# Transposing a batch step's five softmax tiles in one TensorE session of two 64-row tiles, with wide PSUM evictions

## The chip, the core and the metric

The kernel runs on one core of one Trainium2 chip. The metric is the time of one execution on the device in microseconds (us); the kernel before takes 783.63 us, the median of three runs (782.31 to 784.8).

## What is computed

Two independent problems, A and B, are computed and their outputs joined along the last axis. Each is a grouped-query attention block on bf16 data: batch 16, 80 query rows, model width 576, 32 query heads on 16 key/value heads, 512 cached keys, head width 128.

```
q = (x @ wq).reshape(B, Sq, Hq, Dh).transpose(0, 2, 1, 3)
k, v = jnp.repeat(k_cache, 2, axis=1), jnp.repeat(v_cache, 2, axis=1)
p = softmax(einsum("bhqd,bhkd->bhqk", q, k) * Dh ** -0.5, axis=-1)
o = einsum("bhqk,bhkd->bhqd", p, v)
out = o.transpose(0, 2, 1, 3).reshape(B, Sq, Hq * Dh) @ wo
```

## The kernel before

The work is cut into 128 batch steps (U in the code; 64 a problem). A batch step takes one batch entry and four key/value heads. Each key/value head serves two query heads of 80 rows, so it has 160 query rows; the first 128 of them make one score tile of 128 x 512 (k = 1 to 4 in the code, one a head), and the four remainders of 32 rows are put together into a fifth tile (k = 0). So there are 5 x 128 = 640 score tiles.

A tile goes through these stages:

- **QK** on TensorE into a score bank of PSUM: line 658 for k = 1 to 4, and lines 644 to 647 for k = 0, where four matmuls work in four 32-column tiles of the array side by side. Two batch steps' k = 0 tiles are done in one such session.
- **Maximum** on VectorE (line 667), **exponential** with the row sum on ScalarE (line 671, from PSUM to a P tile in SBUF), **reciprocal** of the row sums on VectorE (line 677), **normalisation** of P on GpSimd (line 680).
- **Transposition** of P: four 128x128 TensorE transposes into one PSUM bank (line 686), and one 512-column copy on VectorE from there to pT (line 692 for k = 0, line 694 for k = 1 to 4). For 62 of the 128 batch steps the k = 0 tile is transposed by a DMA from SBUF to SBUF that SyncE issues (line 698).
- **PV** on TensorE (line 731): four matmuls of 160 columns a head, accumulated over the keys; ScalarE copies the result of two heads to oT (line 747).

Around that, TensorE makes the Q projection (line 540: five matmuls of 160 or 480 columns a piece, evicted on ScalarE or VectorE, lines 551 and 552) and the output projection (line 781: 16 matmuls of 288 columns a piece, evicted by lines 793 and 809). K is transposed by DMA on its way in (line 612) and V is loaded plainly (line 616), both issued by SyncE, as are the other loads and the stores.

The order of the instructions on each engine isn't written by hand. Every operation is handed to a planner (`S.add`) with an engine (or two to choose from), a due time in units of one score tile, an estimated duration and, for PSUM, a class of banks. The planner simulates the engines by these estimates, picks the operation that is due first among those that are ready, assigns the banks, and then works out the semaphore waits. An engine runs its list strictly in that order. `BANKS` (line 38) says which of the eight PSUM banks a class may have: S for score tiles, T for transposed tiles, O for PV, M for the projections. `LA` is how many tiles ahead QK runs; `NPA`, `NPR` and `NPT` are the numbers of buffers of P (k = 1 to 4), P (k = 0) and pT.

Of the kernel before, what the change touches and what calls it, by code (L numbers as in the profile page):

```python
# [6 lines left out]
BF16 = mybir.dt.bfloat16  # L7
# [9 lines left out]
NPA = 8  # L17
NPR = 4
NPT = 3
# [28 lines left out]
RDC = 0.78  # L48
RDK = 3.0
RDO = 6.0  # L50
RDD = 1.2
PTO = 0.0
OEO = 0.0
OVO = 0.0
# [19 lines left out]
def _mm(n, cols):  # L74
    return n * (cols * MM1 + MM0)
# [248 lines left out]
def bass_concat_heads__gqa_block_cached__gqa_block_cached__near_ridge_kernel(  # L324
# [9 lines left out]
    B, SQ, D = A_x.shape  # L334
# [12 lines left out]
    NROW = 8 * SQ  # L347
# [4 lines left out]
    with ExitStack() as es:  # L352
        block = es.enter_context(nc.Block())
        sb = lambda name, shape, dt: es.enter_context(nc.sbuf_tensor(name, shape, dt))
        ident = sb("ident", [128, 128], BF16)
# [14 lines left out]
        ps = es.enter_context(nc.psum_tensor("ps", [128, 8, 512], F32))  # L370
        psb = ps[:].bitcast(BF16)
# [3 lines left out]
        sem_names = (["e_pe", "e_act", "e_dve", "e_pool", "d_x00", "d_x01", "d_x10", "d_x11", "d_wo",  # L375
                      "d_wq0", "d_wq1", "d_wqs", "d_wqt"]
                     + ["d_out%d" % i for i in range(NOSB)]
                     + ["d_r%d" % i for i in range(NPT)]
                     + ["d_k%d" % i for i in range(NK)] + ["d_v%d" % i for i in range(NV)])
# [32 lines left out]
        def em_warmend(e):  # L412
# [4 lines left out]
              name="warm", stream="W", dur=NWARM * 0.427, alloc=[vw])  # L417
# [3 lines left out]
        def em_warm2(e, vw=vw2):  # L421
            last = None
            for _ in range(NWARM2):
# [71 lines left out]
        for goct in range(NG):  # L495
            prob, q, half = unit(goct)
# [29 lines left out]
            for i in range(8):  # L526
                for c in range(2):
# [35 lines left out]
                    S.add(("act", "dve"), x + 0.4, em_qev, reads=[R(vb, 0)],  # L563
# [39 lines left out]
        for U in range(NSU):  # L603
# [20 lines left out]
            rdma = RDMA[0] <= U < RDMA[1] and U % 4 in RPER and not any(a_ <= U < b_ for a_, b_ in RSKIP)  # L624
            for k in range(5):
# [7 lines left out]
                tq = Q - LA + 0.0  # L633
                vb = S.bank("S")
                vt = S.bank("T")
# [37 lines left out]

                rg = [g_ for g_ in RG[rdma] if k in g_][0]

# [7 lines left out]
                def em_tr(e, psl=psl, vt=vt):  # L683
                    last = None
                    for j in range(4):
                        last = e.transpose(psb[:, vt.phys, j * 128:(j + 1) * 128],  # L686
                                           p_sb[:, psl, j * 128:(j + 1) * 128], ident[:])
                    return last

                def em_ptev(e, k=k, gl=gl, vt=vt, pts=pts):  # L690
                    if k == 0:
                        return e.tensor_copy(pT[:, pts, :, 4, :],  # L692
                                             psb[:, vt.phys, 0:512].rearrange("p (j n) -> p j n", j=4))
                    return e.tensor_copy(pT[:, pts, :, 0:4, gl * 32:gl * 32 + 32],  # L694
                                         psb[:, vt.phys, 0:512].rearrange("p (j h c) -> p j h c", j=4, h=4))

                def em_rtr(e, psl=psl, pts=pts):
                    return e.dma_start_transpose(pT[:, pts, :, 4, :], p_sb[:, psl, :])

                pt_writes = [R(("pT", pts, g4, "R"), U) for g4 in range(4)] if k == 0 else [R(("pT", pts, gl, "A"), U)]  # L700
# [12 lines left out]
                if k == 0 and rdma:  # L713
                    S.add("sp", max(tg + RDK, 5.0 * (U - NPT) + 7.0), em_rtr, reads=[R(("P", psl), ("n", T))], writes=pt_writes, dsem="d_r%d" % pts,
                          name="rtr%d" % T, stream="RT", dur=RDD, cost=RDC, ahead=RDO)
                else:
                    S.add("pe", t0, em_tr, reads=[R(("P", psl), ("n", T)), IDENT], writes=[R(vt, 0)],
                          name="tr%d" % T, stream="T", dur=_mm(4, 128), lat=0.2, alloc=[vt])
                    S.add("dve", t0 + 0.44, em_ptev, reads=[R(vt, 0)], writes=pt_writes,
                          name="ptev%d" % T, stream="ptev", dur=0.33, lat=0.13, ahead=PTO)  # L720

                if k >= 1:
                    if gl % 2 == 0:
                        vo = S.bank("O")
                    off = (gl % 2) * 160
                    pr = gl // 2

                    def em_pv(e, gl=gl, vo=vo, off=off, vs=vs, pts=pts):
                        last = None
                        for j in range(4):  # L730
                            last = e.matmul(ps[:, vo.phys, off:off + 160],  # L731
                                            lhsT=v_sb[:, vs, gl, j * 128:(j + 1) * 128],
                                            rhs=pT[:, pts, j, :, gl * 32:gl * 32 + 32], start=(j == 0), stop=(j == 3))
                        return last

                    S.marks[4 * U + gl] = S.add(
                          "pe", t0 + 2.5, em_pv,
                          reads=[R(("V", vs), U), R(("pT", pts, gl, "A"), U), R(("pT", pts, gl, "R"), U)],
                          writes=[R(vo, 0)], name="pv%d.%d" % (U, gl), stream="PV",
                          dur=_mm(4, 160), lat=0.2, alloc=[vo] if gl % 2 == 0 else [])  # L740
                    if gl % 2 == 1:
                        hb = 8 * (q % 2) + 4 * pr

                        def em_oev(e, vo=vo, hb=hb, row=half * NROW + bl * SQ):
                            dst = oT[:, hb:hb + 4, row:row + SQ]
                            src = ps[:, vo.phys, 0:320].rearrange("p (h s) -> p h s", h=4)
                            return e.copy(dst, src)  # L747

                        S.add("act", t0 + 3.1, em_oev, reads=[R(vo, 0)],
                              writes=[R(("oT", half, bl, q % 2, pr), (prob, q // 2))], name="oev%d.%d" % (U, pr),  # L750
                              stream="oev", dur=0.33, ahead=OEO)

# [142 lines left out]
```

## Time and profile before

| | |
|---|---|
| three runs | 782.31, 783.63 and 784.8 us |
| the profiled execution's own time | 784.8 us |
| its span, first to last instruction | 784.8 us |
| instructions | 21118 |
| bytes read from HBM, written to it | 87.46 MB, 2.95 MB |
| busy on TensorE, VectorE, ScalarE, GpSimd | 771.8, 674.6, 611.4, 432.4 us |

In the profile PE is TensorE's matmuls (a transpose is one), PEld its weight loads, DVE VectorE, ACT ScalarE, POOL GpSimd and SPq SyncE's queue. A row of the groups reads: line, engine, operation, what it writes and reads, shapes, how many; then busy us and mean ns of one; then how long the engine sat idle just before these instructions, and who ended that. A row of the timeline reads: start in us, how long it lasts, engine, line, what it does, how many in a row. Instructions of one engine overlap in the pipeline, so a row's duration is longer than the distance to the next start.

### The profile page before, as it was taken

How to read it: one execution, taken by the hardware profiler on the slowest of the kernel's cores; microseconds unless marked ns; L12 is line 12 of the kernel's file. 1: busy time of each engine (PE TensorE's matmuls, PEld its weight loads, DVE VectorE, ACT ScalarE, POOL GpSimd, SP SyncE). 2: the span in 40 equal slices, each digit the busy share in tenths (PEclk: the TensorE clock that was granted, in tenths of full speed). 3: DMA queues.
4: the chain of work that ended last, by engine and by line, in shares of the span. 5: the costliest groups of instructions: out<-in, count | busy, mean ns of one | idle time of the engine just before them, and what ended most of it. 6: DMA issues, size and time to landing. Idle time of an engine off the chain costs nothing.

```text
span 784.8 us, 21118 instructions
## 1 busy us (share of the span) xinstructions
PE 771.8 (98%) x8010; PEld 563.8 (72%) x8010; DVE 674.6 (86%) x1559; ACT 611.4 (78%) x1735; POOL 432.4 (55%) x647
## 2 busy tenths in 40 slices
PE   9999999999999999999999999899999999999998
PEld 5576677777777777777777777576777777777787
DVE  4999988888888889899889999797878888988982
ACT  1878988888888889777778778777887887887770
POOL 1455755565655566555565555564555655655660
PEclk9999999999999999999999999999999999999999
DMA  9999999979999999999999999999999998999951
GB/s 250 232 255 243 240 220 252 204 175 205 223 198 225 208 256 273 246 218 221 207 178 219 208 194 229 247 223 218 230 200 210 201 233 203 256 226 188 209 144 32
DMA packets 395812, 168.67 MB, mean 215 GB/s; under 512 B 309824, under 2 KB 392256, under 8 KB 395712
## 3 DMA queue, kind: packets, MB, share of 16 engines
q1 hardware_dynamic: 394496, 166.14, 97.3%
q8 instruction: 65, 1.06, 0.6%
q10 hardware_dynamic: 1216, 1.18, 0.5%
q14 instruction: 35, 0.29, 0.1%
HBM read 87.46 MB, written 2.95 MB: 115 GB/s over the span
## 4 chain that ended last, share of the span: by engine, by line
PE 89%; DVE 7%; DMA 3%; ACT 1%; SPq 0%; issue 0%; POOL 0%; DVEq 0%
PE ps L540 20%; PE ps L781 19%; PE ps L731 17%; PE ps L686 15%; PE ps L658 12%; DVE negmax L667 4%; PE ps L644 4%; DVE pT L694 2%; DMA pT<-p_sb 1%; DMA wo_sb<-in_B_wo_dram 1%; DMA out_dram<-osb 1%; DVE qT L552 1%; ACT p_sb L671 1%; PE ps L409 0%; PE ps L464 0%; PE ps L424 0%
## 5 line engine op out<-in xcount | busy, mean ns | idle before, releaser
L680 POOL TENSOR_SCALAR p_sb<-p_sb,rinv 128x512 bf16<-128x512 bf16 x640 | 430.0, 692 | 331.2 <-DVE rinv L677 330.8
L671 ACT ACTIVATE p_sb<-ps,negmax 128x512 bf16<-128x512 f32 x640 | 441.2, 694 | 76.4 <-DVE negmax L667 66.5
L667 DVE TENSOR_REDUCE negmax<-ps 128x1 f32<-128x512 f32 x640 | 428.3, 679 | 11.6 <-PE ps L658 6.5
L694 DVE COPY pT<-ps 128x512 bf16<-128x512 bf16 x512 | 210.0, 413 | 17.4 <-PE ps L686 15.6
L731 PE MATMUL ps<-pT,v_sb 128*128 128x160 bf16 x2048 | 219.2, 233 | 5.7 <-ACT p_sb L671 4.1
L686 PE MATMUL ps<-ident,p_sb 128*128 128x128 bf16 x2312 | 222.7, 219 | 1.8 <-DVE pT L694 1.2
L540 PE MATMUL ps<-xT,wq_sb 128*128 128x480 bf16 (+1 forms) x1280 | 213.2, 300 | 0.2
L731 PEld LDWEIGHTS ps<-pT,v_sb 128*128 128x128 bf16 x2048 | 158.3, 98 | 58.0 <-ACT p_sb L671 9.7
L686 PEld LDWEIGHTS ps<-ident,p_sb 128*128 128x128 bf16 x2312 | 163.3, 98 | 37.6 <-DVE pT L694 8.5
L658 PE MATMUL ps<-kT,qT 128*128 128x512 bf16 x512 | 189.3, 380 | 0.9 <-ACT p_sb L671 0.9
L781 PE MATMUL ps<-wo_sb,oT 128*128 128x288 bf16 x1280 | 171.6, 286 | 0.5 <-DMA wo_sb<-in_B_wo_dram 0.5
L540 PEld LDWEIGHTS ps<-xT,wq_sb 128*128 128x128 bf16 x1280 | 107.0, 98 | 61.6 <-issue 3.4
L781 PEld LDWEIGHTS ps<-wo_sb,oT 128*128 128x128 bf16 x1280 | 122.5, 98 | 36.5 <-DMA wo_sb<-in_B_wo_dram 1.0
L747 ACT CAST oT<-ps 128x320 bf16<-128x320 f32 x256 | 108.8, 426 | 42.4 <-PE ps L731 41.7
L671 ACT ACTIVATION_READ_ACCUMULATOR p_sb<-ps,negmax 128x1 f32 x640 | 130.7, 204 | 0.0
L551 ACT ACTIVATE qT<-ps 128x160 bf16<-128x160 f32 (+1 forms) x158 | 63.0, 399 | 31.6 <-PE ps L540 30.7
L552 DVE TENSOR_SCALAR qT<-ps 128x480 bf16<-128x480 f32 (+1 forms) x98 | 55.1, 562 | 25.4 <-PE ps L540 24.4
L658 PEld LDWEIGHTS ps<-kT,qT 128*128 128x128 bf16 x512 | 49.3, 98 | 7.5 <-ACT p_sb L671 4.0
L809 DVE TENSOR_TENSOR osb<-ps,acc 128x288 bf16<-128x288 f32 x40 | 18.3, 457 | 29.6 <-PE ps L781 27.8
L677 DVE RECIPROCAL rinv<-rowsum 128x5 f32<-128x5 f32 (+2 forms) x190 | 32.0, 169 | 12.2 <-ACT p_sb L671 12.2
L644 PE MATMUL ps<-kT,qT 128*32 128x512 bf16 x512 | 39.9, 388 | 0.1
L692 DVE COPY pT<-ps 128x512 bf16<-128x512 bf16 x66 | 27.5, 416 | 4.5 <-PE ps L686 4.4
(19 smaller groups left out, 48.7 us busy)
## 6 DMA issues: line engine op xcount, KB each, us to landing
v_sb<-in_A_v_cache_dram SPq DMA_DIRECT2D x64, 512.0 KB, 4.5
v_sb<-in_B_v_cache_dram SPq DMA_DIRECT2D x64, 512.0 KB, 4.6
wo_sb<-in_A_wo_dram SPq DMA_DIRECT2D x8, 576.0 KB, 7.4
wo_sb<-in_B_wo_dram SPq DMA_DIRECT2D x8, 576.0 KB, 7.0
wq_sb<-in_B_wq_dram SPq DMA_DIRECT2D x4, 1024.0 KB, 7.2
out_dram<-osb SPq DMA_DIRECT2D x40, 72.0 KB, 2.4
wq_sb<-in_A_wq_dram SPq DMA_DIRECT2D x2, 1024.0 KB, 7.2
wq_sb<-in_A_wq_dram ACTq DMA_DIRECT2D x2, 512.0 KB, 7.0
```

The costliest lines, as they stand in the source:

```text
L540: last = e.matmul(ps[:, vb.phys, 0:n1 - n0], lhsT=wq_sb[:, wsl, ck, i * 128:(i + 1) * 128], rhs=xT[:, half, ck, n0:n1], start=(ck == 0), s ...
L551: return e.activation(dst, src, AF.Identity, scale=SCALE)
L644: last = e.matmul(ps[32 * g4:32 * g4 + 32, vb_.phys, :], lhsT=qT[:, qsl_, bl_, g4 * 160 + 128:g4 * 160 + 160], rhs=kT[:, ks_, :, g4 * 128: ...
L658: return e.matmul(ps[:, vb.phys, :], lhsT=qT[:, qsl, bl, gl * 160:gl * 160 + 128], rhs=kT[:, ks, :, gl * 128:(gl + 1) * 128], start=True, ...
L667: return e.tensor_reduce(negmax[:, si:si + 1], ps[:, vb.phys, :], axis=AX.X, op=AluOpType.max, negate=True)
L671: return e.activation(p_sb[:, psl, :], ps[:, vb.phys, :], AF.Exp, bias=negmax[:, si:si + 1], scale=1.0, accum_out=rowsum[:, ss, k:k + 1])
L680: return e.tensor_scalar(p_sb[:, psl, :], p_sb[:, psl, :], rinv[:, ss, k:k + 1], 1.0, op0=AluOpType.mult, op1=AluOpType.mult)
L686: last = e.transpose(psb[:, vt.phys, j * 128:(j + 1) * 128], p_sb[:, psl, j * 128:(j + 1) * 128], ident[:])
L694: return e.tensor_copy(pT[:, pts, :, 0:4, gl * 32:gl * 32 + 32], psb[:, vt.phys, 0:512].rearrange("p (j h c) -> p j h c", j=4, h=4))
L731: last = e.matmul(ps[:, vo.phys, off:off + 160], lhsT=v_sb[:, vs, gl, j * 128:(j + 1) * 128], rhs=pT[:, pts, j, :, gl * 32:gl * 32 + 32], ...
L747: return e.copy(dst, src)
L781: last = e.matmul(ps[:, vb.phys, 0:DC], lhsT=oT[:, hi, rb * 128:(rb + 1) * 128], rhs=wo_sb[:, wi, c3 * DC:(c3 + 1) * DC], start=(hi == 0), ...
```

## The change

All five P tiles of a batch step are transposed in one TensorE session; the DMA transposes are gone. Each 128x128 transpose becomes two transposes of 64 rows: the upper 64 partitions of P are transposed in the upper 64 rows of the array, the lower 64 in the lower rows, with `tile_position` (0, 0) and (64, 0). Each has 128 x 64 outputs. They are issued in 20 pairs, one upper and one lower, 40 matmuls a session. The upper halves of the tiles k = 1 to 4 go to one PSUM bank (16 pieces of 64 columns, 1024 bf16 columns), the lower halves to a second, and both halves of the k = 0 tile (512 columns) to a third. The two row tiles must not write one bank at the same time, so the lower halves start with the k = 0 tile and the upper halves end with it; ahead of the 17th pair the session waits on a semaphore that its own fourth pair raises.

Three copies a batch step take the place of five: two of 1024 columns on VectorE, and one of 512 that the planner may give to ScalarE or VectorE. pT is laid out as 16 blocks of 160 columns, so that a PV matmul reads its 160 columns in one run. All PV matmuls of a batch step wait for all three copies. The reciprocals are taken in groups of three and two tiles everywhere.

The constants go along: 12 P buffers for k = 1 to 4 instead of 8, two pT buffers instead of three, three score banks instead of four, and other bank classes and due times.

```diff
-NPA = 8
+NPA = 12
-NPT = 3
+NPT = 2
-BANKS = dict(S=(0, 1, 2, 6), T=(3, 4), O=(5, 7), M=(7, 5), M0=(7, 5, 6, 3, 4), M1=(7, 6), ML=(7, 5, 6, 0, 1))
+BANKS = dict(S=(0, 1, 2), T=(3, 4, 6), Y=(6, 5), O=(5, 7, 4), M=(7, 5, 6, 3, 4), M0=(7, 5, 6, 3, 4), M1=(7, 6), ML=(7, 5, 6, 0, 1))
-RG = (((0, 1, 2, 3, 4),), ((0,), (1, 2, 3, 4)))
-RDMA = (24, 126)
-RPER = (1, 2, 3)
-RSKIP = ((46, 64),)
+RG = ((0, 1, 2), (3, 4))
+TS0 = 4.5
+PV0 = 5.5
+PVS = 0.8
-PTO = 0.0
-OEO = 0.0
-OVO = 0.0
+PTO = -2.0
+PTE = (('dve',), ('dve',), ('act', 'dve'))
+OEO = 3.0
+OVO = 1.0
...
-        pT = sb("pT", [128, NPT, 4, 5, 128], BF16)
+        pT = sb("pT", [128, NPT, 16, 160], BF16)
...
-                def em_tr(e, psl=psl, vt=vt):
-                    last = None
-                    for j in range(4):
-                        last = e.transpose(psb[:, vt.phys, j * 128:(j + 1) * 128],
-                                           p_sb[:, psl, j * 128:(j + 1) * 128], ident[:])
-                    return last
...
-                def em_rtr(e, psl=psl, pts=pts):
-                    return e.dma_start_transpose(pT[:, pts, :, 4, :], p_sb[:, psl, :])
...
+            ts = 5.0 * U + TS0
+            vx, vz, vy = S.bank("T"), S.bank("T"), S.bank("Y")
+
+            def em_tr(e, psls=tuple(psls), vbs=(vx, vz), vy=vy, U=U):
+                last = None
+                for n_ in range(20):
+                    if n_ == 16:
+                        e.wait_ge(sems["e_tr"], U + 1)
+                    for h in range(2):
+                        k_, j = divmod(n_, 4)
+                        k_ = (k_ + 1 - h) % 5
+                        if k_:
+                            c_ = ((k_ - 1) * 4 + j) * 64
+                            dst = psb[:, vbs[h].phys, c_:c_ + 64]
+                        else:
+                            dst = psb[:, vy.phys, 0:512].rearrange("p (g j c) -> p g j c", g=4, j=4)
+                            dst = dst[:, 2 * h:2 * h + 2, j, :]
+                        last = e.matmul(dst, lhsT=p_sb[64 * h:64 * h + 64, psls[k_], j * 128:(j + 1) * 128],
+                                        rhs=ident[64 * h:64 * h + 64, 64 * h:64 * h + 64], start=True, stop=True,
+                                        is_transpose=True, tile_position=(64 * h, 0))
+                    if n_ == 3:
+                        last.then_inc(sems["e_tr"], 1)
+                return last
...
+                def em_ptev(e, en="dve", h=h, vt=vt, pts=pts):
+                    f = e.copy if en == "act" else e.tensor_copy
+                    if h == 2:
+                        return f(pT[:, pts, :, 128:160], psb[:, vt.phys, 0:512].rearrange("p (n c) -> p n c", n=16))
+                    return f(pT[:, pts, :, 64 * h:64 * h + 64], psb[:, vt.phys, :].rearrange("p (n c) -> p n c", n=16))
...
+                                        rhs=pT[:, pts, 4 * gl + j, :], start=(j == 0), stop=(j == 3))
```

More of the change, by code (lines that the diff above doesn't have):

```diff
@@ L623, in bass_concat_heads__gqa_block_cached__gqa_block_cached__near_ridge_kernel @@
             vo = None
-            rdma = RDMA[0] <= U < RDMA[1] and U % 4 in RPER and not any(a_ <= U < b_ for a_, b_ in RSKIP)
+            psls = []
             for k in range(5):
@@ L712, in bass_concat_heads__gqa_block_cached__gqa_block_cached__near_ridge_kernel @@
                       writes=[R(("P", psl), ("n", T))], name="nrm%d" % T, stream="pool", dur=0.674, lat=0.1)
[L713 to L751, printed above, removed]
@@ new lines, in bass_concat_heads__gqa_block_cached__gqa_block_cached__near_ridge_kernel, with em_pv, em_oev @@
+            for gl in range(4):
+                if gl % 2 == 0:
+                    vo = S.bank("O")
+                off = (gl % 2) * 160
+                pr = gl // 2
+                tp = 5.0 * U + PV0 + PVS * gl
+                def em_pv(e, gl=gl, vo=vo, off=off, vs=vs, pts=pts):
+                    last = None
+                    for j in range(4):
+                        last = e.matmul(ps[:, vo.phys, off:off + 160],
+                                        lhsT=v_sb[:, vs, gl, j * 128:(j + 1) * 128],
+                                        rhs=pT[:, pts, 4 * gl + j, :], start=(j == 0), stop=(j == 3))
+                    return last
+                S.marks[4 * U + gl] = S.add(
+                      "pe", tp, em_pv,
+                      reads=[R(("V", vs), U)] + [R(("pT", pts, h), U) for h in range(3)],
+                      writes=[R(vo, 0)], name="pv%d.%d" % (U, gl), stream="PV",
+                      dur=_mm(4, 160), lat=0.2, alloc=[vo] if gl % 2 == 0 else [])
+                if gl % 2 == 1:
+                    hb = 8 * (q % 2) + 4 * pr
+                    def em_oev(e, vo=vo, hb=hb, row=half * NROW + bl * SQ):
+                        dst = oT[:, hb:hb + 4, row:row + SQ]
+                        src = ps[:, vo.phys, 0:320].rearrange("p (h s) -> p h s", h=4)
+                        return e.copy(dst, src)
+                    S.add("act", tp + 0.6, em_oev, reads=[R(vo, 0)],
+                          writes=[R(("oT", half, bl, q % 2, pr), (prob, q // 2))], name="oev%d.%d" % (U, pr),
+                          stream="oev", dur=0.33, ahead=OEO)
```

31 lines of the change are left out of this document (15 added, 16 removed).

## The prediction

> **What bounds the kernel now.** I read the page first: engine totals, the slices' clock and the chain that ended last.
>
> ```profile
> span 784.8 us, 21118 instructions
> ...
> PE 771.8 (98%) x8010; PEld 563.8 (72%) x8010; DVE 674.6 (86%) x1559; ACT 611.4 (78%) x1735; POOL 432.4 (55%) x647
> ...
> PEclk9999999999999999999999999999999999999999
> ...
> PE 89%; DVE 7%; DMA 3%; ACT 1%; SPq 0%; issue 0%; POOL 0%; DVEq 0%
> ```
>
> TensorE is the bound: it is busy for 98% of the span at full clock, idle for 784.8 - 771.8 = 13.0 us, and it owns 89% of the last chain. What the change is worth is therefore what it does to TensorE's queue, plus whatever stalls it adds to the 13 us. A busy TensorE isn't a TensorE at its peak, though, so I then read the timeline, where the start of a group minus the start of the one before is the time that the queue really gives it. TensorE alone first:
>
> ```profile
> 399.81 0.51 PE L540 MATMUL ps<-xT,wq_sb 128*128 128x160 bf16 x5
> 400.16 0.39 PE L686 MATMUL ps<-ident,p_sb 128*128 128x128 bf16 x4
> 400.38 0.44 PE L731 MATMUL ps<-pT,v_sb 128*128 128x160 bf16 x4
> 400.66 0.38 PE L658 MATMUL ps<-kT,qT 128*128 128x512 bf16 x1
> 400.87 0.44 PE L731 MATMUL ps<-pT,v_sb 128*128 128x160 bf16 x4
> ```
>
> Then all engines, at a place with a four-tile session (L644):
>
> ```profile
> 404.57 0.39 PE L686 MATMUL ps<-ident,p_sb 128*128 128x128 bf16 x4
> ...
> 404.80 0.38 PE L658 MATMUL ps<-kT,qT 128*128 128x512 bf16 x1
> ...
> 405.00 0.42 DVE L694 COPY pT<-ps 128x512 bf16<-128x512 bf16 x1 [0.29 <-PE ps L686]
> 405.01 0.44 PE L731 MATMUL ps<-pT,v_sb 128*128 128x160 bf16 x4
> ...
> 405.34 0.68 DVE L667 TENSOR_REDUCE negmax<-ps 128x1 f32<-128x512 f32 x1
> ...
> 405.94 0.41 DVE L694 COPY pT<-ps 128x512 bf16<-128x512 bf16 x1
> 406.00 0.51 PE L540 MATMUL ps<-xT,wq_sb 128*128 128x160 bf16 x5
> 406.06 0.69 ACT L671 ACTIVATE p_sb<-ps,negmax 128x512 bf16<-128x512 f32 x1
> ...
> 406.44 0.62 PE L644 MATMUL ps<-kT,qT 128*32 128x512 bf16 x8
> ...
> 406.73 0.41 ACT L747 CAST oT<-ps 128x320 bf16<-128x320 f32 x1
> 406.87 0.32 DVE L552 TENSOR_SCALAR qT<-ps 128x160 bf16<-128x160 f32 x1
> ...
> 406.99 0.40 PE L686 MATMUL ps<-ident,p_sb 128*128 128x128 bf16 x4
> 407.04 0.70 ACT L671 ACTIVATE p_sb<-ps,negmax 128x512 bf16<-128x512 f32 x1
> 407.11 0.69 DVE L667 TENSOR_REDUCE negmax<-ps 128x1 f32<-128x512 f32 x1
> ```
>
> A P tile's four transposes take 0.23 us of the queue (404.57 to 404.80), 0.0575 each for 128 columns. A QK matmul takes 0.21 for 512 columns (404.80 to 405.01), four PV matmuls 0.28 for 4 x 160 (400.38 to 400.66): each form runs at the same rate per column, so time on TensorE goes by streamed columns. Eight 512-column matmuls in the four 32-column tiles of L644 take 0.55 (406.44 to 406.99) and not 8 x 0.21: tiles side by side share a stream's time. Changing into that mode costs too: the five 160-column matmuls ahead take 0.44 (406.00 to 406.44) where five take 0.35 elsewhere (399.81 to 400.16), 0.09 more, and the session takes 0.55 - 2 x 0.21 = 0.13 over its two streams. A change in and out is 0.22 us.
>
> **The change, part by part.** The other rows that carry terms:
>
> ```profile
> L671 ACT ACTIVATE p_sb<-ps,negmax 128x512 bf16<-128x512 f32 x640 | 441.2, 694 | 76.4 <-DVE negmax L667 66.5 <-DMA pT<-p_sb 2.2 <-PE ps L686 1.2
> ...
> L686 PE MATMUL ps<-ident,p_sb 128*128 128x128 bf16 x2312 | 222.7, 219 | 1.8 <-DVE pT L694 1.2 <-POOL p_sb L680 0.5
> ...
> L694 DVE COPY pT<-ps 128x512 bf16<-128x512 bf16 x512 | 210.0, 413 | 17.4 <-PE ps L686 15.6
> ...
> L686 PEld LDWEIGHTS ps<-ident,p_sb 128*128 128x128 bf16 x2312 | 163.3, 98 | 37.6 <-DVE pT L694 8.5 <-POOL p_sb L680 2.0 <-DVE pT L692 1.1
> ...
> L552 DVE TENSOR_SCALAR qT<-ps 128x480 bf16<-128x480 f32 x71 | 46.5, 656 | 23.4 <-PE ps L540 22.5
> ...
> L551 ACT ACTIVATE qT<-ps 128x480 bf16<-128x480 f32 x57 | 32.4, 568 | 2.2 <-PE ps L540 1.8
> L551 ACT ACTIVATE qT<-ps 128x160 bf16<-128x160 f32 x101 | 30.6, 304 | 29.4 <-PE ps L540 28.8
> ...
> L552 DVE TENSOR_SCALAR qT<-ps 128x160 bf16<-128x160 f32 x27 | 8.5, 317 | 2.0 <-PE ps L540 1.9
> L644 PEld LDWEIGHTS ps<-kT,qT 128*32 128x32 bf16 x512 | 7.8, 94 | 10.9 <-issue 2.6 <-ACT p_sb L671 1.4 <-ACT oT L747 1.3
> ```
>
> *TensorE, removed.* 2312 / 4 = 578 tiles go through L686 now (the other 62 of 640 by DMA): 578 x 0.23 = 132.9 us, all on the path.
>
> *TensorE, added.* 128 sessions, one a batch step, all 640 tiles in them. A session is 20 pairs; each matmul streams 64 columns, one in the upper and one in the lower 64 rows of the array. No row shows row tiles or a 64-column matmul. Low end for a pair: both at once, half of a 128-column step, 0.029. High end: no sharing and no shorter step, 2 x 0.0575 = 0.115. I take 0.029, since L644's session shows that tiles share a stream and every form goes by its columns: 20 x 0.029 + 0.22 for the change of mode = 0.80, x 128 = 102.4 us. **Net -30.5 us**. A weight load stands ahead of each matmul, 40 of 128 columns a session instead of 20. Loads keep up today at one per 0.0575, and one of 128 columns shows 98 ns against 94 for 32 columns, so a load hardly grows with columns; that a new one can follow every 0.029 in each half is my choice, and the first thing that could be wrong. The wait that the session has on its own fourth pair is for a matmul issued 12 pairs (0.35 us) earlier, and one lasts 219 ns by its row: hidden; uncovered it holds the four last pairs, up to 0.1 x 128 = 13 us.
>
> At this place the Trainium skill speaks against the change: "TensorE: Matmul & The Clock Gate", section "Back-to-back issue gap", has starts of matmuls never closer than about 25 ns, however few columns they have. If that holds over both halves together, 40 matmuls take an estimated 1.0 us, a session 1.22, and the 128 sessions 156 us, so +23 in place of -30.5. Its section "Packing small matmuls" has tiles start about 4 ns apart, which would leave my 0.80 nearly as it is. L644's eight matmuls in 0.55 us agree with the second for column tiles; no run here shows row tiles.
>
> *PV.* pT becomes contiguous over a head group's 160 columns. L731 already takes 0.07 for 160 columns beside 0.0575 for 128, the same rate, so nothing is gained; the matmuls stay 2048.
>
> *VectorE.* Removed are 578 copies at 0.34 (405.00 to 405.34): 196 us. Added are 256 copies of 1024 columns. The two L552 rows give (656 - 317) / 320 = 1.06 ns a column and 147 ns fixed; the 512-column bf16 copy, 413, is then 0.52 ns a column; 1024 columns last 0.68, and 0.08 less in the queue (0.42 lasts, 0.34 passes): 0.60, 154 us. (At 1.06 ns a column it would be 1.15, 294 us: then VectorE, not TensorE, sets the time near 784; I take the copy's own row.) By the order of the built kernel reciprocals go from 190 to 256 (+6 at 0.1) and Q evictions from 27 small and 71 large to 62 and 68 (+7). 675 - 196 + 154 + 13 = 646 us, 85% of the new span, as now.
>
> *ScalarE.* It gets 126 of the 128 third copies (512 columns): by the L551 rows 0.825 ns a column and 172 fixed, 0.59, in the queue 0.10 less (406.73 to 407.04 against 0.41) = 0.49, so +62; fewer Q evictions, -6. 611 + 56 = 667, 88% instead of 78%: hidden, but the cover is thinner.
>
> *DMA, SyncE, GpSimd.* 62 P transposes leave SyncE's queue and the DMA engines:
>
> ```profile
> L698 SPq DMA_TRANSPOSE pT<-p_sb x62: 1188/1212/3551, 162.9 to 748.5; - x62
> ```
>
> That is 62 x 1.2 = 75 us of SyncE's queue, which held later K and V loads. The chain has 3% DMA in all, and the one wait that the rows put down to these transposes is 2.2 us of ScalarE's (L671), so I count nothing for their going. The 640 normalisations stay; GpSimd at 55% covers their new grouping.
>
> *Waits added.* Five tiles must be normalised before a session, and all of its three copies done before PV. On the built order the instructions between a session and its first PV are, typically, four QK and 2.0 to 2.4 us of projections, some 2.7 us by the durations above; two copies back to back with a maximum ahead need 0.2 + 0.6 + 1.2 = 2.0. Usually covered, at a few places not. Score banks fall from four to three. A score tile holds its bank from QK to the end of the exponential, 404.80 to 406.06 + 0.69 = 406.75, 1.95 us; three banks at one tile per 758 / 640 = 1.18 us allow 3.55 (four allowed 4.9). I add 4 us of stalls to the 13.
>
> **Sum:** 784.8 - 30.5 + 4 = 758.3 us for an execution like the profiled one. That was the slowest of the three, 1.2 over the median 783.63; against the median the forecast is **757**.
>
> **Rivals.** (a) *Pairs take 0.0575, in the session itself*: either the halves don't share (40 x 0.029), or the weight load sets the step. For it: 40 loads where 20 were, and no load faster than one per 0.0575 in the trace. Against: L644. Price: 20 x 0.0575 + 0.22 = 1.37, 175.4 us, +42.5, so 784.8 + 42.5 + 4 - 1.2 = 830; slower than now. It decides at a pair of (132.9 / 128 - 0.22) / 20 = 0.041 us; between there and 0.0575 lie times of 787 to 830. (b) *The score banks run out*: a tile that meets a third copy on ScalarE (0.49) and both large copies on VectorE (1.2) holds its bank for 1.95 + 1.7 = 3.65, over the 3.55 allowed, and QK stands at the head of TensorE's queue with all else behind it. A quarter of a microsecond a step gives 128 x 0.25 = 32: 785 to 790. Against it: both engines keep over a tenth of the span idle. (c) *No narrowing and no sharing*, so the change does not do what it says: 40 x 0.0575 + 0.22 = 2.52, 322.6 us, +190: about 976. All forms' rate by columns speaks against it.
>
> **How the numbers follow.** Forecast 0.57, with its own range 742 (the stalls gone) to 775 (the wait on the fourth pair, 13, uncovered, and some more stalls); (a) 0.25; (b) 0.13; (c) 0.05. To leave out no more than 2 in 10 the range runs from 742 to 832. A measurement of this kernel can tell about 0.3% (2.4 us) from no change. Faster: 0.57 and a quarter of (b), 0.60. Within it: 0.04, from (b). Slower: (a), (c) and the rest of (b), 0.36.
>
> **What would show it.** The timeline of one session: 0.58 to 0.65 us from first to last of 40 starts is right, over 0.82 (a pair over 0.041) kills the gain. The copies of 1024 columns: 0.68 lasting, 0.60 passing. TensorE's idle time: about 17 us; 40 or more, with QK waiting for the exponential, is (b). The transposes' share of the last chain must fall from 15%. Wrong would be a pair cadence far from 0.029, or idle time in the tens.

## The result, and the profile after

The changed kernel takes 745.88 us (median of four runs, 745.61 to 747.22), the kernel before 784.05 (782.31 to 784.8) on the same chip: a ratio of 0.9528, 95% interval 0.9507 to 0.9549. That is 38.2 us less; the forecast was 757, 26.6 less than the 783.63 it started from. On a second chip the two took 745.11 and 779.49, a ratio of 0.9565 (0.9546 to 0.9583). Times on the chips differ by some 5 us for the kernel before, so the runs below are compared by their ratio to it or with the changed kernel's 745 to 746. One correction ahead: the changed kernel's profiled run took 747.22 us with a span of 745.5, and the other runs stand 1.7 us or more over their spans too. The profiled execution of before, listed with 784.8 for both, so probably took some 786.5 us; its own time isn't on record. Spans are compared with spans here.

The page of the changed kernel: totals, the chain by engine and by line, and the groups that the change made.

```profile
span 745.5 us, 26156 instructions
...
PE 737.5 (99%) x10818; PEld 509.0 (68%) x10818; DVE 649.7 (87%) x1337; ACT 650.1 (87%) x1829; POOL 435.7 (58%) x647
...
PE 96%; DVE 2%; DMA 1%; ACT 1%; issue 0%; SPq 0%
PE ps L537 23%; PE ps L795 21%; PE ps L745 19%; PE ps L655 15%; PE ps L710 11%; PE ps L641 5%; DMA wo_sb<-in_B_wo_dram 1%; DVE negmax L664 1%; ACT p_sb L668 1%; PE ps L406 0%; DVE qT L549 0%; PE ps L461 0%; PE ps L421 0%; DVE pT L727 0%; DVE xT L465 0%
...
L727 DVE COPY pT<-ps 128x1024 bf16<-128x1024 bf16 x256 | 171.0, 682 | 8.7 <-PE ps L710 8.2
...
L710 PEld LDWEIGHTS ps<-ident,p_sb 64*128 64x128 bf16 x5120 | 81.8, 95 | 33.1 <-issue 9.5
L710 PE MATMUL ps<-ident,p_sb 64*128 64x64 bf16 x5120 | 96.9, 190 | 0.0
...
L726 ACT COPY pT<-ps 128x512 bf16<-128x512 bf16 x126 | 75.5, 599 | 6.8 <-PE ps L710 6.1
```

The chain by line in the kernel before, for comparison:

```profile
PE ps L540 20%; PE ps L781 19%; PE ps L731 17%; PE ps L686 15%; PE ps L658 12%; DVE negmax L667 4%; PE ps L644 4%; DVE pT L694 2%; DMA pT<-p_sb 1%; DMA wo_sb<-in_B_wo_dram 1%; DMA out_dram<-osb 1%; DVE qT L552 1%; ACT p_sb L671 1%; PE ps L409 0%; PE ps L464 0%; PE ps L424 0%
```

TensorE is still the bound, more purely than before: 96% of the last chain instead of 89%, and idle for 745.5 - 737.5 = 8.0 us instead of 13.0. The transposes fell from 15% of the chain (L686 before) to 11% (L710), and the two projections L537 and L795 now carry 44% of it. VectorE went from 675 to 650 us, ScalarE from 611 to 650.

The timeline of TensorE around one session (start, how long it lasts, line, shapes, how many):

```profile
359.70 0.59 PE L655 MATMUL ps<-kT,qT 128*128 128x512 bf16 x2
360.22 0.76 PE L710 MATMUL ps<-ident,p_sb 64*128 64x64 bf16 x40
360.91 1.19 PE L537 MATMUL ps<-xT,wq_sb 128*128 128x480 bf16 x5
361.94 0.59 PE L655 MATMUL ps<-kT,qT 128*128 128x512 bf16 x2
362.37 0.51 PE L537 MATMUL ps<-xT,wq_sb 128*128 128x160 bf16 x5
```

The session of 40 takes 0.69 us (360.22 to 360.91), and the two QK matmuls ahead of it 0.52 (359.70 to 360.22) where two take 0.43 without a change behind them (361.94 to 362.37). So a session costs 0.69 + 0.09 = 0.78 us. The starts inside it, in ns from the first, upper and lower half in turn:

```
0 3  38 41  67 71  96 100  126 129  155 158  184 187 ...  476 479  505 508  534 537  563 566
```

From the second pair on, a pair follows a pair after 29.2 ns, the halves of a pair 3 to 4 ns apart; in all 128 sessions first and last start are 566 to 568 ns apart. There is no gap ahead of the 17th pair: its wait is hidden.

For the whole span I took every step from one TensorE start to the next against the step of unbroken groups (columns / 2.4 + 2.5 ns: 56 ns at 128 columns, 216 at 512). What is over it where the tiling changes, up to 0.096 us, is the change; the rest is stall.

| us | before | after |
|---|---|---|
| unbroken steps | 747.2 | 694.2 |
| of these the transposes of P | 129.1 | 76.3 |
| changes of tiling | 12.3 | 35.2 |
| stalls | 21.2 | 12.0 |
| ahead of the first start, behind the last | 4.1 | 4.1 |
| span | 784.8 | 745.5 |

The gain is 53.0 of stream, less 22.9 for changes of tiling, and 9.2 of stalls. The first two make 30.1; the prediction had 30.5. It had 4 us more of stalls, and there were 9.2 fewer.

Not all of the 21.2 us in the kernel before is waiting. The clock granted to TensorE was 0.5 from 498.80 to 502.21 us of its span; the stretch began within the longest stall (shown under e1), and the steps behind the stall took twice their time: four PV matmuls 0.49 us (499.40 to 499.89) where they take 0.28 elsewhere. From the end of the stall to the end of the stretch that is an estimated 1.4 us. The mean granted clock of that execution was 0.998, and 1.0 in the changed kernel.

### The profile page after: what moved, and what is told of

It reads as the page before. It is cut to its first block, busy times and chain, and to the rows that moved or that the text cites. A ratio compares the mean times of both kernels' runs of the same rounds, so it can differ in the third digit from the quotient of the medians.

```text
span 745.5 us, 26156 instructions
## 1 busy us (share of the span) xinstructions
PE 737.5 (99%) x10818; PEld 509.0 (68%) x10818; DVE 649.7 (87%) x1337; ACT 650.1 (87%) x1829; POOL 435.7 (58%) x647
## 4 chain that ended last, share of the span: by engine, by line
PE 96%; DVE 2%; DMA 1%; ACT 1%; issue 0%; SPq 0%
PE ps L537 23%; PE ps L795 21%; PE ps L745 19%; PE ps L655 15%; PE ps L710 11%; PE ps L641 5%; DMA wo_sb<-in_B_wo_dram 1%; DVE negmax L664 1%; ACT p_sb L668 1%; PE ps L406 0%; DVE qT L549 0%; PE ps L461 0%; PE ps L421 0%; DVE pT L727 0%; DVE xT L465 0%
## 5 line engine op out<-in xcount | busy, mean ns | idle before, releaser
L664 DVE TENSOR_REDUCE negmax<-ps 128x1 f32<-128x512 f32 x640 | 418.3, 681 | 39.6 <-PE ps L655 20.1
L537 PE MATMUL ps<-xT,wq_sb 128*128 128x480 bf16 (+1 forms) x1280 | 205.8, 300 | 0.6 <-DVE qT L549 0.2
L795 PE MATMUL ps<-wo_sb,oT 128*128 128x288 bf16 x1280 | 181.1, 286 | 2.7 <-DMA wo_sb<-in_B_wo_dram 2.7
L745 PE MATMUL ps<-pT,v_sb 128*128 128x160 bf16 x2048 | 180.6, 233 | 0.0
L727 DVE COPY pT<-ps 128x1024 bf16<-128x1024 bf16 x256 | 171.0, 682 | 8.7 <-PE ps L710 8.2
L795 PEld LDWEIGHTS ps<-wo_sb,oT 128*128 128x128 bf16 x1280 | 122.3, 98 | 44.1 <-DMA wo_sb<-in_B_wo_dram 2.9
L537 PEld LDWEIGHTS ps<-xT,wq_sb 128*128 128x128 bf16 x1280 | 105.8, 98 | 67.5 <-issue 2.2
L668 ACT ACTIVATION_READ_ACCUMULATOR p_sb<-ps,negmax 128x1 f32 x640 | 138.8, 217 | 0.0
L710 PEld LDWEIGHTS ps<-ident,p_sb 64*128 64x128 bf16 x5120 | 81.8, 95 | 33.1 <-issue 9.5
L710 PE MATMUL ps<-ident,p_sb 64*128 64x64 bf16 x5120 | 96.9, 190 | 0.0
L726 ACT COPY pT<-ps 128x512 bf16<-128x512 bf16 x126 | 75.5, 599 | 6.8 <-PE ps L710 6.1
L548 ACT ACTIVATE qT<-ps 128x480 bf16<-128x480 f32 (+1 forms) x126 | 54.9, 451 | 14.8 <-PE ps L537 14.4
L674 DVE RECIPROCAL rinv<-rowsum 128x3 f32<-128x3 f32 (+1 forms) x256 | 41.8, 163 | 9.1 <-ACT p_sb L668 8.8
```

Of the source, the lines that this page charges most:

```text
L537: last = e.matmul(ps[:, vb.phys, 0:n1 - n0], lhsT=wq_sb[:, wsl, ck, i * 128:(i + 1) * 128], rhs=xT[:, half, ck, n0:n1], start=(ck == 0), s ...
L664: return e.tensor_reduce(negmax[:, si:si + 1], ps[:, vb.phys, :], axis=AX.X, op=AluOpType.max, negate=True)
L668: return e.activation(p_sb[:, psl, :], ps[:, vb.phys, :], AF.Exp, bias=negmax[:, si:si + 1], scale=1.0, accum_out=rowsum[:, ss, k:k + 1])
L710: last = e.matmul(dst, lhsT=p_sb[64 * h:64 * h + 64, psls[k_], j * 128:(j + 1) * 128], rhs=ident[64 * h:64 * h + 64, 64 * h:64 * h + 64], ...
L726: return f(pT[:, pts, :, 128:160], psb[:, vt.phys, 0:512].rearrange("p (n c) -> p n c", n=16))
L727: return f(pT[:, pts, :, 64 * h:64 * h + 64], psb[:, vt.phys, :].rearrange("p (n c) -> p n c", n=16))
```

## The experiments

**Theory 1:** the gain is the shared stream of the two row tiles, less the changes of mode; the stalls went with the DMA transposes of P. **Theory 2:** the stalls went because five tiles are batched and copied in wide pieces. **Theory 3:** batching and wide copies are the gain, not the row tiles. All kernels are compared with the kernel before on their chip, and the changed kernel's ratio to that is 0.953 to 0.957.

### The row tiles alone taken back (e2_full_rows)

```diff
-                for n_ in range(20):
-                    if n_ == 16:
-                        e.wait_ge(sems["e_tr"], U + 1)
-                    for h in range(2):
...
+                for n_ in range(20):
+                    k_, j = divmod(n_, 4)
+                    k_ = (k_ + 1) % 5
...
+                    last = e.transpose(dst, p_sb[:, psls[k_], j * 128:(j + 1) * 128], ident[:])
...
-                  dur=0.59, lat=0.2, alloc=[vx, vz, vy], mode=2)
+                  dur=_mm(20, 128), lat=0.2, alloc=[vx, vz, vy])
```

> The changed kernel, with the session's 40 transposes of 64 rows replaced by 20 of 128 rows on the whole array: same banks, same three copies of 1024, 1024 and 512 columns, no change of mode, no wait inside the session. Theory 1 (the gain is the shared stream of the two row tiles): a session takes 20 x 0.056 = 1.12 instead of 0.60 + 0.19 = 0.79 us, 128 x 0.33 = +43, near 788. Theory 3 (the gain is the batching and the wide copies): within 5 us of the changed kernel, 746 to 751.

785.89 us, ratio 1.0063 (1.0034 to 1.0092). The session in its timeline of TensorE:

```profile
362.39 1.28 PE L706 MATMUL ps<-ident,p_sb 128*128 128x128 bf16 x20
363.50 0.59 PE L655 MATMUL ps<-kT,qT 128*128 128x512 bf16 x2
```

1.11 us (362.39 to 363.50) instead of 0.78: 128 x 0.33 = 42 us, and the time is 40 over the changed kernel's. The two large copies write eight blocks of 128 columns here instead of 16 of 64; all other constants are those of the changed kernel. Batching, wide copies, the third copy on ScalarE, the other constants and the absence of DMA transposes together don't make the kernel faster than before: it is some 5.5 us slower, with 13.7 us more to stream for the 62 tiles that the DMA had. Theory 3 falls.

### The kernel before without its DMA transposes (e1_before_no_dma)

```diff
-RDMA = (24, 126)
+RDMA = (0, 0)
```

> The kernel before with its 62 DMA transposes taken back to TensorE; nothing else. Theory 1 (the stalls that went with the change, 21.2 to 12.0 us between TensorE's starts, came from the DMA transposes of P): 62 x 0.225 = 13.9 us more stream, 9 us fewer stalls, so about +5 us, near 789, and the stalls fall to some 12 us. Theory 2 (the stalls went because five tiles are batched and copied in wide pieces): +14 to +16, 798 to 800, the stalls stay at 20 us or more.

788.67 us, ratio 1.0111 (1.0086 to 1.0136), 8.3 us over its kernel before (780.38): between the +5 of theory 1 and the +14 to +16 of theory 2. The stream grew by 13.7 us (747.2 to 760.9), so 5.4 us came back elsewhere by the medians (3 to 7 by the interval); in its trace the stalls are 9.4 us, against 21.2 in the profiled execution of before, the longest of its runs on that chip. Here the tile-by-tile copies are all in place, 640 of them on VectorE, and the stalls are as low as in the changed kernel: theory 2 isn't needed. What batching, wide copies and the other constants add is seen against e2, which streams the same columns on the same chip: 785.89 to 788.67, 2.8 us. The runs also lie closer together, 788.43 to 790.05, than those of the kernel before on that chip, 778.44 to 783.77.

Where the stalls lay is seen in the kernel before. First its timeline around TensorE's longest stall, then its chain in order of time (start, length, what) and its timeline around the third longest, 38 us later:

```profile
490.52 6.13 SPq L612 DMA_TRANSPOSE kT<-in_B_k_cache_dram  x1
...
496.75 1.21 SPq L698 DMA_TRANSPOSE pT<-p_sb  x1
...
499.40 0.69 PE L731 MATMUL ps<-pT,v_sb 128*128 128x160 bf16 x4 [2.88 <-ACT p_sb L671]
...
499.89 0.63 PE L658 MATMUL ps<-kT,qT 128*128 128x512 bf16 x1
```

```profile
525.84 8.28 DMA pT<-p_sb
```

```profile
534.14 0.69 ACT L671 ACTIVATE p_sb<-ps,negmax 128x512 bf16<-128x512 f32 x1 [2.23 <-DMA pT<-p_sb]
534.20 0.71 PE L731 MATMUL ps<-pT,v_sb 128*128 128x160 bf16 x8 [0.93 <-issue]
```

The transpose issued at 525.84 is in flight until 534.12, and PV starts at 534.20. The one issued at 496.75 lands at 499.31, and PV starts 0.09 later. Four stalls of PV, 3.05, 1.43, 1.09 and 0.83 us, 6.4 together, end 0.09 us behind such a landing. The rows name ScalarE or "issue" for them; no row of TensorE names these transposes. In three of the four the transpose was itself issued late: at 496.75, 580.02 and 720.17 it follows within 0.1 us a transpose of K (L612) with which SyncE was busy for 6.13, 4.37 and 4.24 us. The one issued at 525.84 spent its time in flight.

### The DMA transposes issued, and nobody reads them (e12_dma_unawaited)

```diff
+                if k == 0 and 24 <= U < 126 and U % 4 in (1, 2, 3) and not 46 <= U < 64:
+                    def em_rtr(e, psl=psl):
+                        return e.dma_start_transpose(scr[:, :, :], p_sb[:, psl, :])
+
+                    S.add("sp", max(tg + 3.0, 5.0 * (U - 3) + 7.0), em_rtr, reads=[R(("P", psl), ("n", T))],
+                          writes=[R(("scr",), U)], dsem="d_r", name="rtr%d" % T, stream="RT", dur=1.2, cost=0.78,
+                          ahead=6.0)
```

> The changed kernel, which also issues the 62 DMA transposes of the kernel before, at the same due times, into a scratch buffer that nothing reads; TensorE transposes all tiles as in the changed kernel. It tells apart how these transposes cost the kernel before its stalls. If only because PV waited for their landing: no change, a ratio to the kernel before of 0.953 to 0.957 and stalls of 8 to 13 us. If because they hold SyncE's queue and the DMA engines, so that other loads come late: 3 to 9 us more, a ratio of 0.960 to 0.967.

798.66 us, ratio 1.0182 (1.0149 to 1.0216): some 50 us over the changed kernel, far outside both expectations. Its waits, of SyncE's queue, of TensorE and of ScalarE (who waited for whom: us in total, times, longest):

```profile
SPq L695 <- POOL p_sb L678: 35.7, 40, 2.4
```

```profile
PE ps L656 <- ACT p_sb L669: 20.2, 26, 4.8
...
ACT p_sb L669 <- DMA scr<-p_sb: 11.4, 5, 5.3
```

and SyncE's in the kernel before:

```profile
SPq L698 <- POOL p_sb L680: 22.8, 17, 3.1
```

Stalls are 63.8 us; with a granted clock of 0.987, 20.5 us of the span ran at half clock, so at most some 10 of them are lost clock. The run doesn't isolate the queue as it was meant to: nobody reads the scratch buffer, but ScalarE may not write a P buffer again before the transpose has read it. TensorE's longest stall, 5.0 us, is of that kind: the transpose issued at 276.91 lands at 281.04, the exponential that waited 5.29 us for it starts at 281.06, and QK starts at 281.90. A stall of 2.8 us is of the other kind: SyncE is busy with a K transpose and then with one of these (714.16 to 715.37), the store of an output piece goes out behind it at 715.42 and lands at 717.24, VectorE waits for that store, and the session that waits for VectorE starts at 717.78.

How the 50 us divide isn't settled by this. SyncE stood 22.8 us at such transposes in the kernel before too, where the reciprocal of the tile concerned was taken alone; here it is taken together with two others, later.

### The wait inside the session, uncovered (e3_wait_late)

```diff
-                    if n_ == 3:
+                    if n_ == 15:
```

> The changed kernel; the semaphore that the 17th pair waits for is raised by the 16th pair instead of the fourth. The prediction had the wait hidden by the 12 pairs between. Theory 1: TensorE now stands until the 16th pair has ended (190 ns from its start) and its semaphore is seen, some 0.2 to 0.3 us a session less 0.03, on the path: +22 to +35 us, 768 to 781. Rival: other waits take it up, under +5.

773.56 us, ratio 0.9917 (0.9893 to 0.9942), 28 over the changed kernel. Its timeline:

```profile
362.63 1.00 PE L710 MATMUL ps<-ident,p_sb 64*128 64x64 bf16 x40
363.56 1.15 PE L795 MATMUL ps<-wo_sb,oT 128*128 128x288 bf16 x8
```

The session takes 0.93 instead of 0.69 us; in its starts the 17th pair comes 0.255 us behind the last start of the 16th, not 0.026. That is the price here of a wait of TensorE on its own matmul, and in the changed kernel 12 pairs (0.35 us) cover it.

### One more change of tiling (e4_one_more_switch)

```diff
+                    if n_ == 10:
+                        e.transpose(psb[:, vbs[0].phys, 640:768], p_sb[:, psls[3], 256:384], ident[:])
```

> The changed kernel with one more transpose of 128 rows on the whole array in the middle of each session, whose result is overwritten: TensorE leaves the row tiles and goes back. Theory 1 (a change in and out costs 0.19 us of TensorE's queue wherever it stands): 128 x (0.19 + 0.056 + 0.01) = +33 us, near 779. Rival (the 0.19 is mostly the wait of a session for its inputs, not the change of mode): 128 x 0.056 = +7, near 753.

777.67 us, ratio 0.9968 (0.9954 to 0.9981), 32 over the changed kernel. The session in the timeline:

```profile
364.13 0.47 PE L712 MATMUL ps<-ident,p_sb 64*128 64x64 bf16 x20
364.53 0.23 PE L702 MATMUL ps<-ident,p_sb 128*128 128x128 bf16 x1
364.69 0.47 PE L712 MATMUL ps<-ident,p_sb 64*128 64x64 bf16 x20
365.09 1.15 PE L797 MATMUL ps<-wo_sb,oT 128*128 128x288 bf16 x8
```

0.96 us (364.13 to 365.09) instead of 0.69: 0.27, of which the transpose's own step is 0.056. So a change out and in is some 0.2 us in the middle of work that waits for nothing. It is the change of tiling that costs, and it is why one session of five tiles pays.

### Narrow copies (e6_narrow_copies)

```diff
-                    return f(pT[:, pts, :, 64 * h:64 * h + 64], psb[:, vt.phys, :].rearrange("p (n c) -> p n c", n=16))
+                    for n0 in (0, 8):
+                        last = f(pT[:, pts, n0:n0 + 8, 64 * h:64 * h + 64],
+                                 psb[:, vt.phys, n0 * 64:n0 * 64 + 512].rearrange("p (n c) -> p n c", n=8))
+                    return last
```

> The changed kernel with each 1024-column copy cut into two of 512 columns, one behind the other on VectorE. 256 more instructions of some 0.07 us fixed cost: VectorE +17 us, to some 667 of 746 us busy. If TensorE alone is the bound, as the prediction has it: within 3 us of the changed kernel. If the width of the copies carries part of the gain: +10 to +17 us.

747.3 us, ratio 0.9525 (0.9475 to 0.9575): no difference. The copies keep VectorE busy for 189.1 us instead of 171.0, as expected, but the planner gave 17 Q evictions fewer to it, so VectorE rose by 5.8 us (649.7 to 655.5) and ScalarE by as much (650.1 to 655.9). The extra load was thus shared out; shared out, it costs nothing while TensorE is the bound. What 17 us more on VectorE alone would have done isn't shown.

### Two score banks (e5_two_score_banks)

```diff
-BANKS = dict(S=(0, 1, 2), T=(3, 4, 6), Y=(6, 5), O=(5, 7, 4), M=(7, 5, 6, 3, 4), M0=(7, 5, 6, 3, 4), M1=(7, 6), ML=(7, 5, 6, 0, 1))
+BANKS = dict(S=(0, 1), T=(3, 4, 6), Y=(6, 5), O=(5, 7, 4), M=(7, 5, 6, 3, 4), M0=(7, 5, 6, 3, 4), M1=(7, 6), ML=(7, 5, 6, 0, 1))
```

> The changed kernel with two score banks instead of three (bank 2 goes unused). Rival (b) of the prediction said that score banks run out when a tile holds its bank longer than banks x the time per tile. A tile's hold was 1.95 us or more in the profile before; two banks at 745.5 / 640 = 1.165 us a tile allow 2.33 us, three allow 3.5. If the hold decides, TensorE stalls in QK and ScalarE and VectorE run the chain: at a hold of 2.5 us a tile would take 1.25 us, some 800 us; above 780 in any case. If the planner's order can hide it, within 10 us of the changed kernel.

943.63 us, ratio 1.2029 (1.1934 to 1.2125). The waits of TensorE in it:

```profile
PE ps L655 <- ACT p_sb L668: 70.4, 118, 1.4
PE ps L745 <- DVE pT L727: 24.2, 16, 1.8
PE ps L641 <- ACT p_sb L668: 14.4, 11, 1.7
```

and in the changed kernel, with three:

```profile
PE ps L655 <- ACT p_sb L668: 0.5, 2, 0.3
```

The mechanism of rival (b) exists, one bank further down: with two banks QK stands for the exponential, with three it does for 0.5 us. Its price was not what banks x time per tile gives: a tile's hold has a median of 2.39 us in the changed kernel and 2.14 here, and 640 x 2.14 / 2 = 685 is far from 943. Two things that add to it can be named, not priced: the four-tile sessions need two banks at once, and PV waits for the copies (24.2 us in the rows above). Part is clock: it was 0.942, so 109 us of the span ran at half clock, which costs at most 55 of the 198 us over the changed kernel.

### Sessions side by side, and the projection's weights earlier (e7, e9, e11)

```diff
-            k_, s_, r, o = min(((o.pri, o.seq, r, o) for r, o in cand if r <= now + hold[e]), key=lambda x: x[:2])
+            k_, s_, r, o = min(((o.pri - (ADJ if e == "pe" and mode and o.mode else 0.0), o.seq, r, o)
+                                for r, o in cand if r <= now + hold[e]), key=lambda x: x[:2])
```

```diff
-OPX = ((12.0, 1.8), (18.5, 1.45), (18.5, 1.45), (18.5, 1.45))
+OPX = ((12.0, 1.8), (18.0, 1.4), (20.0, 1.4), (18.5, 1.45))
```

The first edit, with ADJ = 5:

> The changed kernel with one more rule in the planner: while TensorE is in a tiled session, a ready session of the other kind goes ahead of whatever was due first. By the built order 46 of the four-tile sessions of the k = 0 scores stand beside a transposing session, instead of 14. A change from one tiling to the other costs 0.096 us and not 0.096 + 0.093, so 32 x 0.096 = 3 us less switching: near 743. Rival: the sessions come earlier or later than is good, and the stalls take it back (746 or more).

749.67 us (745.02 to 751.09), ratio 0.9546 (0.9488 to 0.9605): inconclusive against 0.953 to 0.957. In its trace the changes fell from 35.2 to 32.1 us, as expected, and the stalls rose from 12.0 to 18.0.

Then three kernels together: the changed one again, the second edit alone, and both with ADJ = 3.

> The changed kernel once more, on the chip of the two kernels sent with it, as their base: 744 to 748.

> The changed kernel with other due times for two of the four output projections (starts 18.0 and 20.0 batch steps after their base instead of 18.5 and 18.5, a piece every 1.4 instead of 1.45), so that the weights of problem B have longer to land: the longest stall of TensorE in the changed kernel is 2.9 us, for these weights. If that stall goes and nothing comes for it: 2 to 3 us less than the changed kernel, near 743. Rival: the wait moves to another load or is filled by other stalls, no change.

> The due times of the run before and the rule for tiled sessions standing together, at a smaller preference (3 tile times instead of 5): 31 sessions side by side by the built order, against 14 in the changed kernel and 46 under the preference of 5. If the stalls seen there came from the strong preference: 17 x 0.096 = 1.6 us less switching and 2 to 3 us less stall, 741 to 743. If any preference costs stalls: 746 or more.

745.11, 744.75 and 747.68 us; ratios 0.9565 (0.9546 to 0.9583), 0.9558 (0.9542 to 0.9574) and 0.9596 (0.9581 to 0.9611). The earlier weights gain nothing that can be told: the 2.9 us stall isn't there in the changed kernel's second profile either (stalls 8.6 us). The preference saves changes (33.4 us) and loses more in stalls (14.3). None of them beats the changed kernel.

### Four row tiles (e8_four_row_tiles)

```diff
-                    for h in range(2):
+                    for h in range(4):
...
-                        last = e.matmul(dst, lhsT=p_sb[64 * h:64 * h + 64, psls[k_], j * 128:(j + 1) * 128],
-                                        rhs=ident[64 * h:64 * h + 64, 64 * h:64 * h + 64], start=True, stop=True,
-                                        is_transpose=True, tile_position=(64 * h, 0))
+                        last = e.matmul(psb[:, vbs[h].phys, c_:c_ + 32],
+                                        lhsT=p_sb[32 * h:32 * h + 32, psls[k_], j * 128:(j + 1) * 128],
+                                        rhs=ident[32 * h:32 * h + 32, 32 * h:32 * h + 32], start=True, stop=True,
+                                        is_transpose=True, tile_position=(32 * h, 0))
...
+                    f(pT[:, pts, :, 32 * h:32 * h + 32], psb[:, vt.phys, 0:512].rearrange("p (n c) -> p n c", n=16))
+                    return f(pT[:, pts, 4 * h:4 * h + 4, 128:160],
+                             psb[:, vt.phys, 512:640].rearrange("p (n c) -> p n c", n=4))
...
-BANKS = dict(S=(0, 1, 2), T=(3, 4, 6), Y=(6, 5), O=(5, 7, 4), M=(7, 5, 6, 3, 4), M0=(7, 5, 6, 3, 4), M1=(7, 6), ML=(7, 5, 6, 0, 1))
+BANKS = dict(S=(0, 1, 2), T=(3, 4, 6, 5), O=(7, 5, 4), M=(7, 5, 6, 3, 4), M0=(7, 5, 6, 3, 4), M1=(7, 6), ML=(7, 5, 6, 0, 1))
```

> The changed kernel with four row tiles of 32 rows instead of two of 64: 20 groups of four transposes of 32 columns, each row tile into a PSUM bank of its own (640 columns), four pairs of copies (512 and 128 columns) on either engine, no wait inside. If time goes by streamed columns, as for two tiles (29.2 ns = 64 / 2.4 + 2.5), a group takes 32 / 2.4 + 2.5 = 16 ns, a session 0.35 + 0.19 us, and the stream falls by 128 x 0.26 = 33 us. If four issues of 3.5 ns or a floor near 25 ns set it, a group takes 25 ns or more: 10 us at most. The time itself may rise all the same: a session holds four of the five other banks, and the copies cost more (VectorE and ScalarE were at 87%); I expect 740 to 790.

871.15 us, ratio 1.1091 (1.1012 to 1.1171), far outside the 740 to 790 expected. The session's groups and TensorE's longest wait, by lines:

```profile
L738 PE MATMUL ps<-pT,v_sb 128*128 128x160 bf16 x2048 | 180.7, 244 | 33.4 <-DVE pT L719 22.4 <-ACT pT L719 9.5 <-issue 1.1
...
L704 PE MATMUL ps<-ident,p_sb 32*128 32x32 bf16 x10240 | 105.4, 177 | 22.5 <-issue 12.9 <-ACT oT L754 7.3 <-DVE qT L550 1.5
```

and the starts of one session, in ns:

```
0 3 6 10  39 41 45 48  64 66 70 73  89 91 95 98  114 116 120 123 ...  189 192 195 199
214 220 228 236  245 258 266 275  283 291 300 308  316 325 333 341 ...  575 583 591 600  608
```

The first groups of four follow each other after 25 ns; from the 33rd matmul on each comes 8.33 ns behind the last, 33 ns for four. First to last start is 608 ns (the median of the 128 sessions): the 80 small transposes take longer than the 40, whose 567 ns they were to halve. So there was nothing to gain in the session, and the 125 us over the changed kernel are lost elsewhere. The rows above name 33.4 us in which PV waits, nearly all for the copies, and 22.5 ahead of the transposes; the granted clock was 0.963, so some 64 us of the span ran at half clock, at most 32 us lost. A session holds four of the five banks that are left beside the scores' three, which fits these waits; the rest isn't divided.

## Why the prediction was right, and where it was off

- **TensorE is the bound, time goes by columns: right.** e2 and e4 move the time by what they move in TensorE's queue, within 3 us (42 us by the queue and 40 measured in e2, 35 and 32 in e4); e6 adds load to VectorE and ScalarE and nothing happens. The "full clock" that the prediction read from the page held but for 3.4 us.
- **A pair at 0.029 us, a session at 0.80: right,** 0.0292 and 0.78. The net of stream and changes was -30.5 and is -30.1. That it agrees so closely is in part luck: what was removed was put at 132.9 and is 129.1, what was added at 102.4 and is 99.2 (76.3 and 22.9), so both were some 3 to 4 us too large. Rival (a), a pair of 0.0575, and (c) are out: weight loads of 64 x 128 keep up with 29.2 ns in each half.
- **The Trainium skill's floor of 25 ns** ("TensorE: Matmul & The Clock Gate", "Back-to-back issue gap") doesn't hold over both halves together: starts are 14.6 ns apart on average. It is there for each tile: in the first eight groups of e8 a tile's matmuls of 32 columns, 16 ns by the columns' rule, start every 25 ns.
- **The wait on the fourth pair, hidden: right.** Its price when uncovered was put at up to 0.1 us; e3 shows 0.23 more in the step. That term of the range was sized too small.
- **Copies: right.** 682 ns last where 680 was forecast, ScalarE's 599 where 590. VectorE came to 650 us for 646. ScalarE came to 650 for 667: its term, +56, was sized too large by 17. Narrowing the copies again cost nothing (e6), so their width was not what was gained.
- **Score banks, +4 us of stalls: wrong in sign, and so is the zero for the DMA transposes.** The step that failed is "I count nothing for their going". It took the rows at their word, where 2.2 us of ScalarE's were the only wait for these transposes. Four PV stalls of 6.4 us in the same trace end at their landings and are put down to ScalarE and to "issue". Three banks cost 0.5 us of waiting, though a tile's hold was sized too small: it was read as 1.95 us off one tile, and the median in the changed kernel is 2.39. The going of the DMA transposes is worth 5.4 us by e1's medians. The span came out 12.8 us under the forecast (758.3 to 745.5): 13.2 from the stalls (-9.2 instead of +4), less 0.4 from the net (-30.1 instead of -30.5); 1.4 of the 13.2 is the half clock behind the longest stall. The measured 745.88 lies near 742, the low end of the forecast's own range, which the prediction had put down to "the stalls gone". If the profiled execution took 786.5 us, the step from it to the median is 2.9 and not 1.2, and the forecast would have been 755.
- **What stays open:** e1 returns 5.4 us by medians, the table has 9.2 between one profile and another, and the kernel before's runs spread over more than 5 us. Three of the four stalls that end at a landing go back to SyncE's queue, one to the time in flight; how the remaining stalls divide isn't shown. e12 costs 50 us by both ways together and doesn't separate them.

## What to carry to other kernels

When the streaming engine is the bound, count what it streams: a transpose streams as many columns as its identity is wide, so two 64-row halves at once halve it, provided enough of them stand in one session to pay 0.19 us for the change of tiling in and out. Copies elsewhere only have to stay covered. A transfer in a shared DMA queue can come late by what stands ahead of it, delays what stands behind it, and keeps its source buffer until it has landed; e12 paid 50 us for 62 transposes that nobody read. A row that names an engine long done as the releaser is to be checked against landings.

## What the runs showed of the hardware that was not expected

- A change between the whole array and row or column tiles costs 0.096 us going in and 0.093 going out; from one tiling straight to the other it is 0.096 once (the session at 115.94 us of the changed kernel, right behind a four-tile session).
- With four row tiles of 32 columns (e8), a tile got a new weight load and matmul every 25 ns in the first eight groups, and all tiles together got one every 8.33 ns behind them; why isn't shown. Two tiles of 64 columns, at 29.2 ns a pair, are slower than both and showed neither limit.
- TensorE waiting on its own matmul: 0.255 us from that matmul's start to the next one's (e3).
- With TensorE stalled more often, the granted clock fell: 0.942 in e5, 0.963 in e8, 0.987 in e12, 0.998 in the kernel before, 1.0 in the changed kernel. It falls in stretches of 3.4 us or two to three times that, at half clock. In the kernel before the one stretch began within its 3.05 us stall; the changed kernel's stall of 2.9 us brought none.
